# Full-height float32r products, with the weights' high and low parts on the two halves of the lanes, for the state products of the second four batches

## The chip, the cores and the metric

The kernel runs on one core of a Trainium2 chip. The metric is the device time of one execution in microseconds, the median of several runs. The time before is 1491.74 us, the median of 3 runs (1489.16 to 1493.12).

## The reference

Three layers follow each other, all in float32.

- Bidirectional attention between 8 batches of 512 tokens (`x`, 8 heads of 64) and, for each batch, 32 state rows (`state`, the same heads). Each token reads the states (softmax over the 32 states, then `a @ state`), and each state reads the tokens (softmax over the 512 tokens, then `a2 @ x`).
- A gated feed-forward layer on the 4352 rows that come out: `(silu(x @ w_gate) * (x @ w_val)) @ w_out`, 512 to 1536 to 512.
- A second one: `h = x @ w_in`, `(h * sigmoid(1.702 h)) @ w_out`, 512 to 2048 to 512.

What the tokens read is `a @ state` (per head), and the next layer multiplies it with `w_gate` and `w_val`. The kernel multiplies the states with those weights first, per batch and head: `a @ (state_h @ w_h)`, where `w_h` is the 64 rows of the weight that belong to head h.

## The kernel before, in words

**Exactness by parts.** The products are made in float32r, a form of float32 that TensorE multiplies in one pass. A number is split into a high part (a cast to float32r) and a low part (the number less its high part), and a product is the sum of three matmuls: high x high, low x high, high x low (`mm_rows`, L327 to L332; `mm_acc`, L339 to L342). Where plain float32 is used instead, a matmul is recorded as two instructions.

**Order of the work.** The first stage goes through nine blocks of tokens: batches 0 to 6, then the 256 state rows, then batch 7. For each block there are twelve steps f = 0 to 11 (128 columns of the 1536 each), written out by hand in `run`: the product for the gate (`product`, L974), Silu on ScalarE (L977), whatever is planned for place 0; the product for the value (L986), its multiplication with the Silu on VectorE (L992), whatever is planned for place 1; the split of the result h (`cut`, L797 on ScalarE and L798 on VectorE), the twelve output matmuls of the step before (`out1(f - 1)`, L952 to L954), whatever is planned for place 2. At f = 0 there is no step before, so there are no output matmuls. A product of a token block is six matmuls of 128 x 128 by 512 columns (L330 to L332, twice). Each engine works through its instructions in the order in which they are written here.

**Jobs.** For every batch the products `state_h @ w_h` are made once. This goes by fours: the states of four batches stand side by side as the 128 columns of the stationary operand (`quad_t[qd]`, 64 lanes for each of the two heads of a pair). A job `quad_job(qd, u, k)` multiplies them with a weight tile of two heads (128 lanes x 512 columns: u counts 256 columns of gate and of value, k the four pairs of heads). The two heads of a pair stand on the two halves of the lanes, so a job is two plain float32 matmuls of 64 lanes (L629), one for each half, into two PSUM tiles. There are 24 jobs for each four. Those of the first four are made in block 0. Those of the second four are made in blocks 1, 2 and 3, eight in each, at place 0 of f = 1, 2, 3, 5, 6, 7, 10 and 11 (`job_places`, L681: place n is f = n // 3, place n % 3). The two PSUM tiles are copied into one tile "qs" by ScalarE (L635) and VectorE (L636), and stored to DRAM two places later by a DMA that ScalarE issues (`move`, L652). Of the second four's jobs every third takes its "qs" tile from a ring of two kept for that, the others from a ring of four tiles named "raw" (RAWS = 4), which weights and results of blocks also use. The products are fetched per batch (`fetch`, L661, issued by ScalarE) and split by `cut_fetched`, high on ScalarE (L667) and low on GpSimd (L668), a step or two before the product that uses them.

**The second four's states** are turned at place 0 of f = 0 of block 1: `turn_states(1)`, four transposes into PSUM (L383) and a copy by VectorE into `quad_t[1]` (L385). There too the last block's results leave PSUM (L808, L809).

**Attention pieces** of the next batch lie between (`GROUP`, L58 to L71): transposes of x on TensorE (L432), copied by ScalarE (L440) and reduced to the low part by VectorE (L445), at place 1 of f = 0, 1, 5 and 6; scores (L452 to L455) at f = 1 and 6, places 1 and 2; `cut_x` on GpSimd (L481) at f = 2 and 7; `state_sum` (L582 to L591) after f = 4 and 9.

Of the kernel before, what the change touches and what calls it, by code (L numbers as in the profile page):

```python
# [9 lines left out]
F32R = mybir.dt.float32r  # L10
U32 = mybir.dt.uint32
ACTF = mybir.ActivationFunctionType
ALU = mybir.AluOpType
# [61 lines left out]
def kernel(  # L75
# [26 lines left out]
    DM = H * D  # L102
    FF1 = w_gate.shape[1]
    FF2 = w2_in.shape[1]
    P = 128
    KD = DM // P
# [4 lines left out]
    HP = H // 2  # L111
# [4 lines left out]
    v, a, pe, pool_e, sy = nc.vector, nc.scalar, nc.tensor, nc.gpsimd, nc.sync  # L116
# [4 lines left out]
    work = ctx.enter_context(tc.tile_pool(name="work", bufs=2))  # L121
# [5 lines left out]
    late = ExitStack()  # L127
# [3 lines left out]
    ap = early.enter_context(tc.tile_pool(name="attn", bufs=1))  # L131
# [4 lines left out]
    def f32(t):  # L136
        return t.bitcast(F32)
# [13 lines left out]
    whole = {}  # L151
# [4 lines left out]
    pos = {"dma": 0, "begun": 0, "done": 0, "ahead": 4, "outs": 0, "jobs": 0}  # L156
    RAWS = 4
# [127 lines left out]
    def need_whole(key):  # L285
        while pos["done"] <= where[key]:
            before = pos["done"], pos["begun"]
            whole_slot()
            assert before != (pos["done"], pos["begun"]), key
# [57 lines left out]
    def gv():  # L347
        return psg.tile([P, 512], F32, name="gv", tag="gv")
# [3 lines left out]
    def at():  # L352
        if extra:
            extra.append(extra.pop(0))
            if extra[0] != "at":
                return psa.tile([P, 512], F32, name="at", tag=extra[0])
        return pst.tile([P, 512], F32, name="at", tag="at")
# [3 lines left out]
    stc = ap.tile([P, HP, 2, 64], F32R, name="stc")  # L361
    v.memset(f32(stc), 0.0)
    quad_t = {}
    HALVES = [(slice(0, 64), slice(0, 32)), (slice(64, 128), slice(32, 64))]
    sread = dp.tile([NT, DM], F32, name="sread")

# [12 lines left out]
    def turn_states(qd):  # L379

        ps = at()
        for hp in range(HP):
            pe.transpose(ps[:, hp * P : (hp + 1) * P], sb["raw"][:, hp, :], ident)  # L383
        quad_t[qd] = t = ap.tile([P, HP, P], F32, name="qt", tag="qt", bufs=2)
        v.tensor_copy(t, ps.rearrange("p (k m) -> p k m", k=HP))  # L385

    def attn_state(b):
        t = quad_t[b // 4][:, :, b % 4 * NS : b % 4 * NS + NS]
        for r, c in HALVES:
            if b < 2:  # L390
                src = t[r].rearrange("p (g q) m -> p g q m", g=2)
                a.copy(sts[b][r, :, 0:3:2, c], src)
            else:
                a.copy(stc[r, :, 1, c], t[r])
        if b > 1:
            for r, c in HALVES:
                v.tensor_tensor(stc[r, :, 0, c], t[r], f32(stc[r, :, 1, c]), op=ALU.subtract)
# [222 lines left out]
    def quad_job(qd, u, k, late=False):  # L620


        if qd == 0:
            need_whole(("gv", u, k))
        w = whole[u * KD + k]
        ps = [at(), at()]
        for hl in range(2):
            r = slice(hl * 64, hl * 64 + 64)
            pe.matmul(ps[hl], quad_t[qd][r, k], w[r], start=True, stop=True)  # L629
        pos["jobs"] += 1  # L630
        if qd == 0 and not late or pos["jobs"] % 3 == 0:
            t = ap.tile([P, 2, DM], F32, name="qs", tag="qs", bufs=2)
        else:
            t = work.tile([P, 2, DM], F32, name="qs", tag="raw", bufs=RAWS)
        a.copy(t[:, 0], ps[0])  # L635
        v.tensor_copy(t[:, 1], ps[1])  # L636
        g, q = divmod(k, 2)
        skip = NS * (1 - qd)
        if q == 0:
            quads[qd, u, g] = dp.tile([4 * (P - skip), DM], F32, name=f"sw{qd}_{u}_{g}")  # L640
        rows = quads[qd, u, g].rearrange("(q h p) m -> q p h m", q=2, h=2)
        moved[qd].append((rows[q], t[skip:]))
        if qd == 0 and u >= OWN:
            if q == 0:
                sw[0, u, g] = x_tiles(xp, u % 2 * 2 + g, DM)
            for hl in range(2):
                r = slice(q * 64 + hl * NS, q * 64 + hl * NS + NS)
                sy.dma_start(f32(sw[0, u, g][0][r]), t[:NS, hl])

    def move():  # L650
        for to, t in moved.pop(0):
            a.dma_start(to, t)  # L652
        moved.append([])
# [17 lines left out]
    def job_places(b):  # L671

        if b == 0:
            own = [-2, 0, 1, 2]
            first = [(n, 0, k) for k, n in enumerate((0, 1, 2, 3))]
            last = [(n, 1, k) for k, n in enumerate((28, 30, 32, 34))]
            return [(n, 0, u, k) for n, u, k in first + last] + [
                (6 * (u - 1) + own[k], 0, u, k) for u in range(OWN, U1) for k in range(KD)
            ]
        if b < 4:  # L680
            return [(n, 1, *divmod(8 * (b - 1) + j, KD)) for j, n in enumerate((3, 6, 9, 15, 18, 21, 30, 33))]  # L681
        return []

    def plan_weights(plan, i):


        b = order1[i]
        nb = order1[i + 1] if i + 1 < NB1 else None
        if nb == B:
            nb = None  # L690

        def put(f, place, fn, *args):
            plan.setdefault((f, place), []).append(lambda: fn(*args))

        for n, qd, u, k in job_places(b):
            put(n // 3, n % 3, quad_job, qd, u, k, n >= 3 * F1 - 6)
        for g in range(2):
            if 0 < b < B:
                put(b == 1, g, cut_fetched, b, 1, g)
                if b == 1:  # L700
                    put(0, g + 1, fetch, b, 1, g)
                for u in range(2, U1):
                    put(2 * u - 3, g + 1, fetch, b, u, g)
                    put(2 * u - 2 + (b == B - 1), g + (b < B - 1), cut_fetched, b, u, g)
            if nb is not None:
                put(9, g, fetch, nb, 0, g)
                put(10, g, cut_fetched, nb, 0, g, (ae, f"a{g}") if b == B else None)
                if nb > 1:
                    put(11, g, fetch, nb, 1, g)
# [21 lines left out]
    def plan_batch(plan, b):  # L731

        G0 = groups[b, 0]
        G1 = groups[b, 1] = Group(b, 1, {"xn": "xc1"} if b < 2 else None, b < 2)

        def load_next():
            if b + 1 < B:
                groups[b + 1, 0] = Group(b + 1, 0)
                if b + 1 == 2:
                    load_states(1)  # L740
                groups[b + 1, 0].load()

        named = {"A0": A0, "A1": A1, "G0": G0, "G1": G1}
        more = {"attn_state": lambda: attn_state(b), "next": load_next}
        if b == 1:
            for key, words in BLOCK0.items():
                plan[key] = [piece(w, named, more) for w in words.split()]
            return
        plan[0, 0] = [lambda: attn_state(b)]
        if b == 2:  # L750
            plan[0, 0].append(lambda: turn_states(1))
        for g, f0, then in (("G0", 0, G1.load), ("G1", 5, load_next)):
            for (f, place), words in GROUP.items():
                fns = [then if w == "next" else piece(f"{g}.{w}", named, more) for w in words.split()]
                plan.setdefault((f0 + f, place), []).extend(fns)
        plan.setdefault((5, 0), []).append(G0.state_store)
        plan.setdefault((10, 0), []).append(G1.state_store)
# [42 lines left out]
    def x_tiles(pl, k, N):  # L800
        t = pl.tile([P, 2, S], F32R, name="xo", tag=f"x{k}")
        return t[:, 0, :N], t[:, 1, :N]
# [24 lines left out]
    def warm():  # L827
# [3 lines left out]

    more = {
        "attn_state": lambda: (turn_states(0), attn_state(0)),
        "slot": whole_slot,
        "sw0": lambda: state_weights(0, 0),
# [65 lines left out]
    for i, blk in enumerate(order1):  # L901
# [5 lines left out]
        if blk + 1 < B:  # L907
            plan_batch(plan, blk + 1)
        plan_weights(plan, i)
        if i == NB1 - 3:  # L910
            plan.setdefault((F1 - 2, 2), []).append(load_tail)
# [358 lines left out]
    for n in range(len(order2)):  # L1270
        N = NT if order2[n] == B else S
        for f in range(F2):
# [14 lines left out]
            ps = gv()  # L1287
# [43 lines left out]
```

## Time and profile before

| what | value |
|---|---|
| median of 3 runs | 1491.74 us (1489.16 to 1493.12) |
| the profiled execution | 1492.28 us |
| its span, first to last instruction | 1490.5 us |
| granted clock of TensorE, mean over the span | 0.997 of 2.4 GHz |
| TensorE busy | 1467.6 us, 7688 matmuls |
| VectorE, ScalarE, GpSimd busy | 915.6, 684.2, 396.1 us |
| data moved by DMA | 269.30 MB, mean 181 GB/s |

PE is TensorE's matmuls, PEld its weight loads (which overlap with matmuls), DVE is VectorE, ACT is ScalarE, POOL is GpSimd, SP is SyncE; a q behind an engine's name is its sequencer. Times of a timeline are microseconds from the start of the span. Matmuls are pipelined: one shown with 0.40 us lets the next start after a little over half of that, so what a matmul costs is read from start to start. In a timeline, instructions of one line that follow each other are merged into one row (x4).

### The profile page before, as it was taken

To read this page: it belongs to the slowest core of one execution; us is meant where nothing else is said; L and a number is where in the kernel's file an instruction comes from. 1 tells how busy PE (TensorE), PEld (TensorE's weight loads), DVE (VectorE), ACT (ScalarE), POOL (GpSimd) and SP (SyncE) were. 2 spreads that over 40 slices of the span, in tenths; PEclk is the share of its full clock that TensorE was granted. 3 is DMA by queue.
4 is the path that set the end of the run, shared out by engine and by line. 5 is a ranking of instruction groups with operands and counts; after the bars stand their busy time and mean duration, and the time that the engine had idled before them with its cause. 6 is when DMAs were issued, how large, how long until landed. Compare 5 with 4: busy or idle time off the path is not lost.

```text
span 1490.5 us, 21226 instructions
## 1 busy us (share of the span) xinstructions
PE 1467.6 (98%) x7688; PEld 1193.8 (80%) x7688; DVE 915.6 (61%) x1600; ACT 684.2 (46%) x1247; POOL 396.1 (27%) x325
## 2 busy tenths in 40 slices
PE   7999999999999999999999999999999999999998
PEld 4445677777787777898788889999999999999997
DVE  7985565656678787943344335656565665656554
ACT  6766554555566666654444333333333232323322
POOL 2665221222234445477646330000000000000000
PEclk9999999999999999999999999999999999999999
DMA  7975433333365656425657746565654646574653
GB/s 217 292 248 159 133 99 110 108 125 105 126 189 172 197 170 190 130 100 171 207 189 270 261 147 211 180 232 174 209 198 170 240 159 240 178 240 165 207 183 128
DMA packets 138480, 269.30 MB, mean 181 GB/s; under 512 B 46728, under 2 KB 57992, under 8 KB 138376
## 3 DMA queue, kind: packets, MB, share of 16 engines
q1 hardware_dynamic: 114680, 223.64, 45.5%
q10 hardware_dynamic: 23696, 44.31, 8.9%
q8 instruction: 61, 1.00, 0.3%
q14 instruction: 43, 0.35, 0.1%
HBM read 202.11 MB, written 63.70 MB: 178 GB/s over the span
## 4 chain that ended last, share of the span: by engine, by line
PE 84%; DMA 5%; DVE 4%; ACT 3%; issue 2%; POOL 1%; SPq 0%; ACTq 0%; DVEq 0%; POOLq 0%
PE acc L340 8%; PE acc L341 8%; PE acc L342 8%; PE acc L952 5%; PE acc L954 5%; PE gv L330 5%; PE acc L953 5%; PE gv L331 4%; PE gv L332 4%; DMA xf<-sw 4%; PE gv L1232 4%; PE gv L1231 4%; PE gv L1230 4%; PE at L629 4%; PE at L1230 3%; PE at L1231 3%
## 5 line engine op out<-in xcount | busy, mean ns | idle before, releaser
L798 DVE TENSOR_TENSOR h<-sg,h 128x512 fp32r<-128x512 f32 (+1 forms) x240 | 193.5, 806 | 129.8 <-ACT h L797 128.2
L797 ACT CAST h<-sg 128x512 fp32r<-128x512 f32 (+1 forms) x251 | 149.8, 597 | 170.4 <-DVE sg L1264 80.2
L340 PE MATMUL acc<-wo,h 128*128 128x512 f32 x512 | 200.6, 392 | 0.0
L341 PE MATMUL acc<-wo,h 128*128 128x512 f32 x512 | 200.6, 392 | 0.0
L342 PE MATMUL acc<-wo,h 128*128 128x512 f32 x512 | 199.2, 389 | 0.0
L1254 ACT ACTIVATE sg<-wt 128x512 f32<-128x512 f32 x56 | 35.4, 632 | 299.5 <-DVE wt L1252 299.5
L668 POOL TENSOR_TENSOR xo<-xf,xo 128x512 fp32r<-128x512 f32 x84 | 110.9, 1325 | 231.9 <-ACT xo L667 216.5
L952 PE MATMUL acc<-h,wu 128*128 128x512 f32 (+1 forms) x428 | 165.9, 388 | 0.1
L954 PE MATMUL acc<-h,wu 128*128 128x512 f32 (+1 forms) x428 | 163.8, 383 | 2.0 <-DVE h L798 2.0
L953 PE MATMUL acc<-h,wu 128*128 128x512 f32 (+1 forms) x428 | 163.4, 382 | 0.0
L330 PE MATMUL gv<-a,xo 128*128 128x512 f32 x336 | 137.3, 409 | 0.0
L331 PE MATMUL gv<-a,xo 128*128 128x512 f32 x336 | 133.9, 399 | 0.6 <-POOL xo L668 0.5
L332 PE MATMUL gv<-a,xo 128*128 128x512 f32 x336 | 133.0, 396 | 0.0
L992 DVE TENSOR_TENSOR sg<-gv,sg 128x512 f32<-128x512 f32 (+1 forms) x107 | 70.5, 659 | 83.1 <-PE gv L332 50.7
L342 PEld LDWEIGHTS acc<-wo,h 128*128 128x128 f32 x512 | 96.2, 188 | 20.8
L340 PEld LDWEIGHTS acc<-wo,h 128*128 128x128 f32 x512 | 96.6, 189 | 17.1
L341 PEld LDWEIGHTS acc<-wo,h 128*128 128x128 f32 x512 | 96.6, 189 | 15.8
L1252 DVE TENSOR_TENSOR wt<-wt,gv 128x256 f32<-128x256 f32 x56 | 23.6, 421 | 136.4 <-PE gv L1232 136.4
L952 PEld LDWEIGHTS acc<-h,wu 128*128 128x128 f32 x428 | 80.9, 189 | 22.1 <-issue 6.1
L977 ACT ACTIVATE sg<-gv 128x512 f32<-128x512 f32 (+1 forms) x108 | 61.5, 570 | 80.1 <-PE gv L332 77.0
L954 PEld LDWEIGHTS acc<-h,wu 128*128 128x128 f32 x428 | 80.9, 189 | 21.1 <-DVE h L798 5.5
L1232 PE MATMUL gv<-xo,wu 128*128 128x256 f32 x336 | 95.4, 284 | 0.0
(178 smaller groups left out, 3438.6 us busy)
## 6 DMA issues: line engine op xcount, KB each, us to landing
wo<-w2b SPq DMA_DIRECT2D x128, 512.0 KB
wc<-w2c SPq DMA_DIRECT2D x84, 512.0 KB
xf<-sw ACTq DMA_DIRECT2D x84, 256.0 KB
raw<-in_moe_w_out_dram SPq DMA_DIRECT2D x28, 512.0 KB
sw<-qs ACTq DMA_DIRECT2D x24, 512.0 KB
sw<-qs ACTq DMA_DIRECT2D x24, 384.0 KB
xn<-in_x_dram SPq DMA_DIRECT2D x16, 512.0 KB
y<-ev SPq DMA_DIRECT2D x16, 512.0 KB
```

The costliest lines, as they stand in the source:

```text
L330: pe.matmul(ps, wh, xh, start=k == 0, stop=False)
L331: pe.matmul(ps, wl, xh, start=False, stop=False)
L332: pe.matmul(ps, wh, xl, start=False, stop=k == len(pairs) - 1)
L340: pe.matmul(ps, lh, rh, start=first, stop=False)
L341: pe.matmul(ps, lh, rl, start=False, stop=False)
L342: pe.matmul(ps, ll, rh, start=False, stop=last)
L797: a.copy(h_, src)
L798: eng.tensor_tensor(l_, src, f32(h_), op=ALU.subtract)
L952: pe.matmul(ps, w[:, 0, c], h[:, 0, :N], start=f == 0, stop=False)
L953: pe.matmul(ps, w[:, 1, c], h[:, 0, :N], start=False, stop=False)
L954: pe.matmul(ps, w[:, 0, c], h[:, 1, :N], start=False, stop=f == F1 - 1)
L1232: pe.matmul(ps, w[:, 0, c], x_[:, 1, kt], start=False, stop=kt == 1)
```

## The change

The jobs of the second four batches are made as float32r matmuls of full height. The 64 rows of a head's weight appear twice on the 128 lanes: the high part on the head's own half, the low part on the other half. The states of that head appear twice as well, once on each half, as high parts (`sh`) and as low parts (`sl`). One matmul with `sh` gives high x high + high x low, one with `sl` low x high + low x low. So a job becomes four matmuls of 128 lanes, two for each head, in place of two plain float32 matmuls of 64 lanes.

`turn_states(1)` makes `sh` and `sl`, each 128 lanes x 1024 numbers, by four ScalarE copies and four VectorE subtractions over 64 lanes x 512; they take the two "qs" tiles, which the second four's jobs then no longer use: all their results go to the ring "raw". A new function `cut_job`, planned two places before each job (place 1 of f - 1), makes the weight's parts in another tile of that ring: two copies of 64 lanes x 512 by ScalarE and two subtractions by GpSimd, the second of each for the other head. The jobs of the first four stay as they were.

```diff
@@ -361,6 +361,8 @@
     v.memset(f32(stc), 0.0)
     quad_t = {}
+    quad_parts = []
+    job_parts = {}
...
@@ -383,6 +385,15 @@
         quad_t[qd] = t = ap.tile([P, HP, P], F32, name="qt", tag="qt", bufs=2)
         v.tensor_copy(t, ps.rearrange("p (k m) -> p k m", k=HP))
+        if qd == 1:
+            sh, sl = (ap.tile([P, HP, 2, P], F32R, name="qp", tag="qs", bufs=2) for _ in range(2))
+            for hl in range(2):
+                own, other = (slice(64 * x_, 64 * x_ + 64) for x_ in (hl, 1 - hl))
+                for r in (own, other):
+                    a.copy(sh[r, :, hl], t[own])
+                for r in (own, other):
+                    v.tensor_tensor(sl[r, :, hl], t[own], f32(sh[own, :, hl]), op=ALU.subtract)
+            quad_parts.extend((sh, sl))
...
@@ -624,11 +635,16 @@
         w = whole[u * KD + k]
         ps = [at(), at()]
+        wc = job_parts.pop((u, k)) if qd else None
         for hl in range(2):
             r = slice(hl * 64, hl * 64 + 64)
-            pe.matmul(ps[hl], quad_t[qd][r, k], w[r], start=True, stop=True)
+            if qd == 0:
+                pe.matmul(ps[hl], quad_t[qd][r, k], w[r], start=True, stop=True)
+                continue
+            for n, part in enumerate(quad_parts):
+                pe.matmul(ps[hl], part[:, k, hl], wc[:, hl], start=n == 0, stop=n == 1)
         pos["jobs"] += 1
-        if qd == 0 and not late or pos["jobs"] % 3 == 0:
+        if qd == 0 and (not late or pos["jobs"] % 3 == 0):
             t = ap.tile([P, 2, DM], F32, name="qs", tag="qs", bufs=2)
...
@@ -647,6 +663,14 @@
+    def cut_job(u, k):
+        w = whole[u * KD + k]
+        job_parts[u, k] = t = work.tile([P, 2, DM], F32R, name="wc", tag="raw", bufs=RAWS)
+        for hl in range(2):
+            own, other = (slice(64 * x_, 64 * x_ + 64) for x_ in (hl, 1 - hl))
+            a.copy(t[own, hl], w[own])
+            pool_e.tensor_tensor(t[other, hl], w[own], f32(t[own, hl]), op=ALU.subtract)
+
...
@@ -693,6 +717,8 @@
         for n, qd, u, k in job_places(b):
+            if qd == 1:
+                put((n - 2) // 3, (n - 2) % 3, cut_job, u, k)
             put(n // 3, n % 3, quad_job, qd, u, k, n >= 3 * F1 - 6)
```

## Rows read from the trace of the kernel before

**Rows 1.** The page: busy time by engine, and the chain that ended last.

```profile
PE 1467.6 (98%) x7688; PEld 1193.8 (80%) x7688; DVE 915.6 (61%) x1600; ACT 684.2 (46%) x1247; POOL 396.1 (27%) x325
...
PE 84%; DMA 5%; DVE 4%; ACT 3%; issue 2%; POOL 1%; SPq 0%; ACTq 0%; DVEq 0%; POOLq 0%
```

**Rows 2.** Windows, blocks 1 and 3: stretch, length, each engine's busy time (instructions), clock, DMA.

```profile
154.00:240.00 86.00, 85.53 (x369) 61.89 (x368) 53.70 (x90) 44.18 (x77) 22.65 (x17) 1.00 0.33 111
...
325.00:412.00 87.00, 87.00 (x379) 64.02 (x378) 54.29 (x91) 43.77 (x77) 21.27 (x16) 1.00 0.38 129
```

**Rows 3.** Groups by line, TensorE, 154 to 412: count | busy us, mean ns | idle.

```profile
L629 PE MATMUL at<-wf,qt 64*128 64x512 f32 x96 | 32.4, 639 | 0.0
```

**Rows 4.** Timeline around an ordinary job (f = 6, block 1): start, length, instruction.

```profile
199.83 0.40 PE L332 MATMUL gv<-a,xo 128*128 128x512 f32 x1
...
200.54 0.40 PE L332 MATMUL gv<-a,xo 128*128 128x512 f32 x1
200.87 1.13 PE L629 MATMUL at<-wf,qt 64*128 64x512 f32 x4
...
201.93 0.50 PE L330 MATMUL gv<-a,xo 128*128 128x512 f32 x1
...
202.26 0.40 PE L331 MATMUL gv<-a,xo 128*128 128x512 f32 x1
```

**Rows 5.** Timeline around a long job (f = 5, block 1), TensorE and VectorE.

```profile
192.25 1.25 DVE L587 TENSOR_TENSOR low<-at,low 64x128 f32<-64x128 f32 x4 [0.38 <-ACT low L582]
...
192.66 0.39 PE L332 MATMUL gv<-a,xo 128*128 128x512 f32 x1
192.98 1.76 PE L629 MATMUL at<-wf,qt 64*128 64x512 f32 x4
...
194.67 0.49 PE L330 MATMUL gv<-a,xo 128*128 128x512 f32 x1
```

**Rows 6.** Single lines, 154 to 412: count, shortest/median/longest ns, first and last start, shape.

```profile
L668 POOL TENSOR_TENSOR xo<-xf,xo x36: 1265/1288/1312, 167.2 to 401.9; 128x512 fp32r<-128x512 f32 x36
...
L481 POOL TENSOR_TENSOR xc<-xn,xc x12: 1289/1570/1737, 177.2 to 384.8; 128x512 fp32r<-128x512 f32 x12
...
L454 ACT COPY ST<-at x12: 581/582/583, 167.7 to 377.5; 64x512 f32<-64x512 f32 x12
...
L455 DVE TENSOR_TENSOR ST<-at,ST x12: 682/683/685, 168.3 to 378.1; 64x512 f32<-64x512 f32 x12
```

**Rows 7.** Timeline of the start of block 1, up to its first job.

```profile
160.09 0.69 DVE L385 COPY qt<-at 128x512 f32<-128x512 f32 x1
...
161.01 0.59 ACT L440 CAST xth<-at 128x512 fp32r<-128x512 f32 x1 [1.86 <-PE at L432]
...
162.30 1.20 PE L629 MATMUL at<-wf,qt 64*128 64x512 f32 x4
```

**Rows 8.** Timeline of the start of block 2, up to its first job.

```profile
247.63 0.59 ACT L440 CAST xth<-at 128x512 fp32r<-128x512 f32 x1 [0.78 <-PE at L432]
...
248.11 0.62 ACT L667 CAST xo<-xf 128x512 fp32r<-128x512 f32 x1
...
248.87 1.27 POOL L668 TENSOR_TENSOR xo<-xf,xo 128x512 fp32r<-128x512 f32 x1 [0.59 <-ACT xo L667]
248.92 1.19 PE L629 MATMUL at<-wf,qt 64*128 64x512 f32 x4
```

**Rows 9.** Timeline of ScalarE before the job of rows 4.

```profile
196.80 0.59 ACT L440 CAST xth<-at 128x512 fp32r<-128x512 f32 x1 [2.08 <-PE at L432]
```

**Rows 10.** Timeline of block 2, f = 7: GpSimd and VectorE at the same time.

```profile
298.73 2.99 POOL L481 TENSOR_TENSOR xc<-xn,xc 128x512 fp32r<-128x512 f32 x2 [3.49 <-ACT xc L480]
298.78 1.79 DVE L798 TENSOR_TENSOR h<-sg,h 128x512 fp32r<-128x512 f32 x1
```

**Rows 11.** Timeline of block 1, f = 1 and 2.

```profile
169.14 0.47 PE L452 MATMUL at<-xth,stc 128*128 128x512 f32 x1 [0.37 <-DVE ST L455]
...
169.80 1.30 POOL L668 TENSOR_TENSOR xo<-xf,xo 128x512 fp32r<-128x512 f32 x1
```

## The prediction

> **What bounds the kernel now.** I read the page first: TensorE is busy 98% of the span, and the chain that ended last lies on it for 84% [rows 1]. The profiled execution took 1492.28 us (span 1490.5), 0.54 us above the median of the three runs; I make the sum against 1492.28 and take 0.5 off at the end. Then the stretches in which the change acts, blocks 1 to 3 of the first stage, 154 to 412 us: TensorE is busy for nearly all of each block, ScalarE for half, GpSimd for a quarter [rows 2]. So here a microsecond taken from TensorE's instructions is a microsecond of the end, one that TensorE waits is lost, and work added to ScalarE or GpSimd is free only while its result is ready when TensorE reaches the job that uses it. That last question decides this case.
>
> **What is removed.** The 24 jobs of these blocks keep TensorE busy for 32.4 us [rows 3]. An ordinary job: matmuls of 512 columns follow each other at 0.237 us (199.83 to 200.54 in three steps); from the last one before the job (200.54) to the second after it (202.26) is 1.72 us, so the job costs 1.72 - 2 x 0.237 = 1.25, which is 0.12 more than its busy 1.13: the edges between half-height and full-height work [rows 4]. All jobs: 32.4 + 24 x 0.12 = 35.3 us. Seven of them are long (1.69 instead of 1.06 from first start to the next line's): the second head's PSUM bank is freed only when VectorE's L587 group ends at 193.50 [rows 5].
>
> **What comes in its place on TensorE**: 96 full-height float32r matmuls of 512 columns, the form of L330 to L332, so 24 x 4 x 0.237 = 22.8 us. Gain 35.3 - 22.8 = **12.5 us**. Against this speaks a rule of the Trainium skill (TensorEngine Tiling (Array Packing), Theoretical Speedup): a contraction of 64 or less gains up to 2x from two row tiles, which the change gives up; a half-height pair side by side here takes 0.53, and if a full-height matmul cost as much, the gain would turn into a loss of some 16 us. The trace does not agree for float32r: L330's takes 0.237.
>
> The long jobs keep part of their wait, since the bank is released by others. In the one shown the job would start 0.09 earlier (no edge), its first two matmuls end at 193.36, and the second pair could start some 0.14 after 193.50: 0.28 us. Over the seven (0.24 to 0.48 each by how long they last) that is **2.4 us** given back; bounds 0 and 3.5.
>
> **What is added**, and where it lies.
> - Each job gets two ScalarE copies and two GpSimd subtractions, each over 64 lanes x 512, two places before the job. No GpSimd row has 64 lanes. GpSimd's full-height subtraction L668 takes 1.288 us in the median; on ScalarE and VectorE half-height rows (L454, L455) cost 0.58 and 0.68, what full-height ones cost (0.59, 0.69) [rows 6, 7]. By these I take 1.29 for GpSimd; bounds are half of it (0.64) if it goes by lanes, and 1.74, the slowest of the pairs L481. Together 48 x 1.29 = 62 us of GpSimd and 48 x 0.58 = 28 us of ScalarE, which fit into their idle time as sums.
> - Once, at the start of block 1, four ScalarE copies and four VectorE subtractions cut the states, between VectorE's L385 and L992.
> - No DMA is added. The fetches that ScalarE issues (L661) go behind the copies, about a microsecond later. The eight products that lay in the tile "qs" go to the ring of four that also takes the weight parts; there a job reuses what the job two before it left, some 14 us earlier, and the store of a product is issued two places behind it. I cost that at nothing; without that cover it would be a store's landing per job.
>
> **When is the weight part ready?** The copies go on ScalarE behind what its place has already, at f - 1, place 1; the job is at f, place 0. Between the two TensorE normally has the twelve output matmuls of place 2 (12 x 0.237 = 2.8 us) and one product (six, 1.4). At f = 6, ScalarE starts L440 at 196.80 [rows 9] and can follow 0.49 later: copies done 197.89 and 198.4, GpSimd (0.14 later, as in [rows 8]) 198.03 to 199.3 and on to 200.6. The second pair is due at 200.87 - 0.09 + 0.475 = 201.25: in time by 0.65. f = 2 and f = 7 are alike, the others looser. **But at f = 0 there are no output matmuls.** So the first job of each block, three in all, comes too early:
> - Block 2: L440 starts at 247.63, the copy follows at 248.12 and ends at 248.72, GpSimd works 248.87 to 250.15 and to 251.45; the second pair then ends at 251.93, where a job with all at hand would end at 248.92 - 0.09 + 0.95 = 249.78 [rows 8]. TensorE loses 2.15 us. Block 3 has the same order and loses 2.4.
> - Block 1: after L385 (ends 160.78) the four state copies hold ScalarE until 162.9, so L440, at 161.01 now, starts at 162.8 and the weight copies at 163.3; VectorE's subtractions run until 164.3; GpSimd works 164.04 to 166.6, or until 166.9 if VectorE holds it up. The job ends near 167.4 instead of 162.30 - 0.09 + 0.95 = 163.16 [rows 7]: 4.25 us.
> Together **8.8 us** lost; by the two bounds of GpSimd's instruction (six of them stand in these waits) 4.9 and 11.5.
>
> What is late next, in block 1 only: GpSimd's second L668 there, now at 169.80, is wanted by the product at f = 2 almost at once [rows 11]. It goes behind one more pair of GpSimd subtractions (2.6 us), while TensorE comes 4.25 later and the DMA that feeds this chain is not as much later. I put 1.5 us of wait, less 0.4 that TensorE now waits before L452 at 169.14 and then no longer would: **1.1 us**, bounds -0.4 and 2.6.
>
> VectorE and GpSimd hold each other up: while GpSimd's pair L481 ran (2.99 us instead of 2 x 1.29), VectorE's L798 took 1.79, where its like alone take 0.69 [rows 10]. VectorE's delays are covered (h is wanted 5 us later). GpSimd's 0.41 per pair eats most of the margin at f = 2, 6 and 7: **0.4 us** over these eight jobs, bounds 0 and 3. The Trainium skill (SBUF — State Buffer, Who interferes with whom) has this as an exclusive lock for a whole instruction, so that one 0.69 us subtraction of VectorE could slip in between the pair: 0.69 instead of 0.41, which would make the 0.4 about 1.0. The row shows less.
>
> **Sum**: 12.5 - 2.4 - 8.8 - 1.1 - 0.4 = -0.2 us: the gain is all but used up. 1492.28 + 0.2, less 0.5 for the median: **1491.9 us**.
>
> **Rivals.**
> - *Faster: the cuts are cheap.* If a half-height GpSimd instruction takes 0.64, the three block starts lose 4.9, L668's wait and the interference vanish: 12.5 - 2.4 - 4.9 = 5.2, 1486.6 us. For it: half the elements. Against it: the half-height rows of the two other engines. 0.14.
> - *Slower: the cuts are late at more than the block starts.* If each takes 1.74 in the middle of VectorE's work, as the slowest of L481 do, the starts lose 2.7 more, L668's wait 0.9, and f = 2, 6 and 7, whose margins I put at 0.65 to 0.9, some 3.9 less the 0.4: 7.1 more, 1499.0 us. It decides from about 1.57 us an instruction (then the loss passes 4.5). For it: L481's median, 1.57. Against it: L668 never exceeds 1.312 beside the same VectorE [rows 6]. 0.17.
> - *The new matmuls are no cheaper than the old*: no gain, but the costs, 1492.28 + 8.8 + 1.1 + 0.4 - 0.5 = 1502 us. Only if float32r products of this kind differ from L330's. 0.04. The skill's rule on row tiles, taken at its word, adds the 16 us named above.
>
> **How the numbers follow.** The forecast, no change that can be told (0.3% is 4.5 us here, about what a measurement can tell), has 0.65; its own range is 1488 to 1496. Faster by over 0.3% is the first rival, 0.14; slower the other two, 0.21. The range reaches to the first two: 1485.5 to 1499.
>
> **What would show it.** Right: L629's line has 96 matmuls of 128 lanes, 0.237 apart, with no edges; TensorE idles before it three times, at f = 1 of blocks 1 to 3, released by GpSimd's subtraction, 4 us once and 2 us twice; GpSimd's new line near 1.29 us; the three blocks together as long as before. Wrong: waits on GpSimd in more than a few other jobs (slower), starts that lose under a microsecond (faster), or the time moving outside these blocks, for which I see no reason.

## The result, and the profile after

The changed kernel takes **1505.93 us** (median; 1503.39 to 1514.12), the one before 1491.71 beside it: ratio 1.0106, 95% interval 1.0089 to 1.0123. It is slower by 14 us. The forecast was no change, 1491.9 us with a range up to 1499.0; the result lies 7 us above the range. The profiled execution took 1506.14 us, its span is 1504.3, the mean granted clock 0.992.

The page of the changed kernel: busy time by engine, and the chain that ended last.

```profile
PE 1462.7 (97%) x7688; PEld 1207.1 (80%) x7688; DVE 934.4 (62%) x1604; ACT 713.1 (47%) x1299; POOL 465.6 (31%) x373
...
PE 70%; DMA 7%; ACT 4%; DVE 3%; issue 2%; POOL 2%; ACTq 0%; SPq 0%; POOLq 0%; DVEq 0%
```

TensorE is busy for 4.9 us less than in [rows 1], but the span is 13.8 longer: TensorE now waits, and its share of the chain falls from 84% to 70%.

Windows of the changed kernel, blocks 1 to 3; the columns are those of [rows 2].

```profile
154.00:240.00 86.00, 76.98 (x340) 60.82 (x340) 58.57 (x90) 52.97 (x93) 44.62 (x33) 0.96 0.32 102
240.00:325.00 85.00, 79.87 (x360) 63.45 (x359) 56.82 (x90) 52.27 (x92) 42.65 (x31) 1.00 0.34 113
325.00:412.00 87.00, 81.87 (x363) 65.10 (x361) 56.60 (x89) 51.25 (x91) 42.65 (x32) 0.98 0.33 110
```

TensorE is idle for 9 us in the first window (0.5 in the same window before), 5 in each of the others. GpSimd works twice as long, ScalarE 7 to 9 us longer, and the clock column falls to 0.96 and 0.98.

**The matmuls are as cheap as forecast.** Timeline of the changed kernel, the job at f = 2 of block 1 (no job waits there):

```profile
176.85 0.39 PE L332 MATMUL gv<-a,xo 128*128 128x512 f32 x1
177.08 1.10 PE L645 MATMUL at<-wc,qp 128*128 128x512 f32 x4
178.02 0.39 PE L330 MATMUL gv<-a,xo 128*128 128x512 f32 x1
```

L645 is the jobs' new line. From its first start to the next line's, 177.08 to 178.02, the job takes 0.94 us and has no edges. Counted as the forecast counts, from the last matmul before the job to the second one behind it, less two (at 0.235), such a job takes 0.927 in place of 1.25; times of jobs below and their excess over 0.927 are counted so.

**What TensorE waits for.** The waits between 150 and 430 us: engine and line, releaser, us in total, times, the longest.

```profile
PE at L645 <- POOL wc L672: 7.7, 6, 3.6
PE at L645 <- ACT qs L651: 5.3, 3, 1.9
PE at L645 <- DVE low L598: 2.1, 2, 1.1
PE gv L331 <- POOL xo L692: 1.7, 1, 1.7
PE at L645 <- ACT xo L691: 1.3, 1, 1.3
PE at L645 <- DVE ST L466: 1.1, 3, 0.4
```

There are four kinds. *The weights' parts at the block starts* (L672 is `cut_job` on GpSimd). Timeline of block 2's first job, ScalarE, GpSimd and TensorE:

```profile
253.15 1.26 ACT L671 CAST wc<-wf 64x512 fp32r<-64x512 f32 x2
...
253.91 2.61 POOL L672 TENSOR_TENSOR wc<-wf,wc 64x512 fp32r<-64x512 f32 x2 [0.66 <-ACT wc L671]
255.22 0.30 PEld L645 LDWEIGHTS at<-wc,qp 128*128 128x128 f32 x2 [1.63 <-POOL wc L672]
255.22 0.73 PE L645 MATMUL at<-wc,qp 128*128 128x512 f32 x2 [1.18 <-POOL wc L672]
...
256.57 0.73 PE L645 MATMUL at<-wc,qp 128*128 128x512 f32 x2 [0.62 <-POOL wc L672]
```

The pair of GpSimd instructions takes 2.61 us; TensorE starts the first half as the first ends, waits again for the second, and the job takes 2.34 us more than 0.927.

*The second halves of jobs* (L651, L598, L691, L466 in the list: PSUM copies and what they stand behind). Timeline of the job at f = 5, block 1, which answers to [rows 5]:

```profile
192.00 2.67 POOL L672 TENSOR_TENSOR wc<-wf,wc 64x512 fp32r<-64x512 f32 x2 [4.39 <-issue]
...
194.75 1.36 POOL L692 TENSOR_TENSOR xo<-xf,xo 128x512 fp32r<-128x512 f32 x1
194.99 1.66 DVE L545 TENSOR_TENSOR a<-aT,a 128x512 fp32r<-128x512 f32 x1
...
197.05 0.63 PE L645 MATMUL at<-wc,qp 128*128 128x512 f32 x2
...
197.43 1.25 DVE L598 TENSOR_TENSOR low<-at,low 64x128 f32<-64x128 f32 x4
197.52 0.62 ACT L691 CAST xo<-xf 128x512 fp32r<-128x512 f32 x1 [1.14 <-DMA xf<-sw]
198.04 0.59 ACT L1003 ACTIVATE sg<-gv 128x512 f32<-128x512 f32 x1
...
198.53 0.58 ACT L651 COPY qs<-at 128x512 f32<-128x512 f32 x1
...
199.25 0.71 PE L645 MATMUL at<-wc,qp 128*128 128x512 f32 x2 [1.58 <-ACT qs L651]
```

Before, the group now at L598 began 0.73 us ahead of the job, now 0.38 after it: VectorE is late. And the second half waits not for that group but for L651, the copy of the job's own *first* half: the two halves have got the same one of the two PSUM tiles (read from the releaser here; the run with strict turns below bears it out). That copy in turn stands in ScalarE's order behind Silu (L1003) and behind L691, which waits 1.14 us for the DMA of the fetched rows; in blocks 2 and 3 it is the same, with 1.50 and 1.38 us.

*`cut_fetched` in block 1* (L692): 1.7 us once.

*A wait that was in no part of the forecast*, at the start of block 4. Timeline of ScalarE and TensorE:

```profile
420.66 0.36 ACTq L676 DMA_DIRECT2D sw<-qs  x1
...
430.11 0.59 ACT L834 COPY ev<-acc 128x512 f32<-128x512 f32 x1 [4.80 <-DMA sw<-qs]
...
432.31 0.60 PE L330 MATMUL gv<-a,xo 128*128 128x512 f32 x1 [2.31 <-DVE sg L1018]
```

The copy of the last block's results wants a tile of the ring of four. It holds the last job's product, whose store was issued at 420.66 and ends only at 430. ScalarE waits 4.80 us, and behind it TensorE.

**The clock.** Windows of three stretches of the changed kernel, with the granted clock behind the engines:

```profile
162.90:169.70 6.80, 4.98 (x11) 3.49 (x12) 2.36 (x4) 3.31 (x6) 5.43 (x4) 0.50 0.19 64
343.80:347.20 3.40, 3.33 (x8) 2.66 (x9) 1.26 (x2) 0.07 (x1) 1.63 (x2) 0.50 0.00 0
432.60:436.00 3.40, 3.40 (x10) 2.51 (x10) 2.75 (x3) 2.48 (x6) 1.86 (x2) 0.51 0.97 280
```

At 0.50 (1.2 of 2.4 GHz) the full-height matmuls start 0.427 us apart in place of 0.233. All three stretches begin in or right behind waits of blocks 1, 3 and 4; a fourth is at 565.7 to 569.1. Before there was none in blocks 1 to 5.

From first result copy to first result copy, block 1 takes 93.81 us (87.05 before), block 2 87.29 (84.87), block 3 88.68 (84.87), block 4 78.81 (75.58), block 5 77.41 (77.32): 16.3 us more. What lies before and behind gives 2.4 back, between two executions.

### The profile page after: what moved, and what is told of

Same layout as the page of the kernel before. It is cut to its first block, busy times and chain, and to the rows that moved or that the text cites. A ratio compares the mean times of both kernels' runs of the same rounds, so it can differ in the third digit from the quotient of the medians.

```text
span 1504.3 us, 21367 instructions
## 1 busy us (share of the span) xinstructions
PE 1462.7 (97%) x7688; PEld 1207.1 (80%) x7688; DVE 934.4 (62%) x1604; ACT 713.1 (47%) x1299; POOL 465.6 (31%) x373
## 4 chain that ended last, share of the span: by engine, by line
PE 70%; DMA 7%; ACT 4%; DVE 3%; issue 2%; POOL 2%; ACTq 0%; SPq 0%; POOLq 0%; DVEq 0%
PE acc L340 8%; PE acc L341 8%; PE acc L342 8%; DMA xf<-sw 5%; PE gv L1258 4%; PE gv L1257 4%; PE gv L1256 4%; PE gv L331 3%; PE gv L332 3%; PE gv L330 3%; PE acc L980 3%; PE acc L979 3%; PE acc L978 3%; PE at L1256 3%; PE at L1257 3%; PE at L1258 3%
## 5 line engine op out<-in xcount | busy, mean ns | idle before, releaser
L692 POOL TENSOR_TENSOR xo<-xf,xo 128x512 fp32r<-128x512 f32 x84 | 115.2, 1376 | 108.5 <-ACT xo L691 98.3
L1003 ACT ACTIVATE sg<-gv 128x512 f32<-128x512 f32 (+1 forms) x108 | 61.7, 571 | 71.2 <-PE gv L332 68.0
```

## The experiments

Diffs are against the changed kernel unless said otherwise. "Second-half wait" is what lies between a job's second and third matmul beyond 0.235 us, from start to start.

**The two halves of the change.** *Without the weights' cuts*; the states' high parts stand in as the moving operand.

```diff
-        wc = job_parts.pop((u, k)) if qd else None
+        wc = quad_parts[0].rearrange("p k h m -> p (k h m)").rearrange("p (h m) -> p h m", h=2) if qd else None
...
-            if qd == 1:
-                put((n - 2) // 3, (n - 2) % 3, cut_job, u, k)
```

> Leaves out the weights' high and low parts altogether: the 96 full-height matmuls of blocks 1 to 3 take the states' high parts as their moving operand too, so the products are not those of the reference; the states are still cut at the start of block 1. Theory A (what cost the time are the cuts: GpSimd's subtractions are late at the block starts and hold VectorE up, so that PSUM banks come free late): no wait on GpSimd before a job, the waits before a job's second half fall from 11.9 us to the 2 to 3 us that the old form had, block 1's start keeps about 2 us for the states' low parts, TensorE's clock stays up, and the time is 13 us of cheaper matmuls less some 5: about 1484 us (1481 to 1487). Theory B (the waits before the second half come from the new matmuls themselves, which reach the bank sooner and at f = 5 share the first half's bank): those waits stay at 8 to 12 us, and the time is 1490 to 1494.

Measured: 1485.2 us, ratio 0.9955 (0.9941 to 0.9969). Blocks 1 to 3 take 86.33, 82.35 and 82.13. So the matmuls alone do gain, 7 us; two costs stay without any weight cut. Its waits, 154 to 412 us:

```profile
PE at L645 <- ACT qs L651: 2.5, 3, 1.0
PE at L645 <- DVE xtl L456: 1.5, 1, 1.5
PE at L645 <- ACT qp L393: 1.0, 1, 1.0
```

The first row is the shared PSUM tile at f = 5 (second-half waits of 0.9 to 1.2 each). The others are block 1's first job behind the states' cut.

*All cuts made, but the products by the old half-height matmuls*:

```diff
-            if qd == 0:
+            if True:
                 pe.matmul(ps[hl], quad_t[qd][r, k], w[r], start=True, stop=True)
```

> All cuts are made, but the jobs go back to the old half-height float32 matmuls, which do not use them. Theory A: no wait on GpSimd's parts at the block starts; the waits before a job's second half rise from 2.5 us toward the changed kernel's 11.9 (VectorE is late by GpSimd's work), and the evacuation at the start of block 4 still waits for the ring: 1497 to 1503 us. Theory B (the new matmuls make the waits): the second halves wait as in the kernel before, and the time is within 3 us of it plus block 4's 2 to 4 us, 1492 to 1496.

Measured: 1504.98 us, ratio 1.0088 (1.0071 to 1.0106), above both. The cuts cost 12 us although no job uses them: long jobs take 2.75 to 3.05 us (1.87 and 2.05 before), those at f = 7 2.05 (1.29), and the first job of block 1 5.77, at half clock. Timeline at f = 5 of block 1 (the old matmuls are L642 here):

```profile
198.47 1.12 PE L642 MATMUL at<-wf,qt 64*128 64x512 f32 x2
...
198.77 1.25 DVE L598 TENSOR_TENSOR low<-at,low 64x128 f32<-64x128 f32 x4
...
200.16 1.09 PE L642 MATMUL at<-wf,qt 64*128 64x512 f32 x2 [0.57 <-ACT sg L1003]
```

VectorE's group begins 0.30 us behind the job, where it began 0.73 ahead of it before, and the second half starts 0.14 after that group's end. So a loss of this size comes about without TensorE waiting for a single weight part, through VectorE, ScalarE and the PSUM tiles.

**One cost at a time.** *A block's first cut in the block before*:

```diff
-            if qd == 1:
+            if qd == 1 and n > 3:
                 put((n - 2) // 3, (n - 2) % 3, cut_job, u, k)
...
+        if b < 3:
+            put(F1 - 1, 1, cut_job, *divmod(8 * b, KD))
```

> Only the cut of each block's first job is moved, to the last step of the block before (f = 11, place 1). Theory A: the waits on GpSimd before the first jobs of blocks 2 and 3 (1.35 + 0.78 us each) are gone, and with them the half clock in block 3; in block 1 the states' low parts, ready near 162.6, still hold the job for about 2 us; 8 to 11 us less than the changed kernel, 1495 to 1498. If the half clock does not follow from these waits but from the work, it stays (7 us of half clock in block 1, 3.4 in block 3) and the gain is 5 to 6 us, 1500.

Measured: 1498.76 us, ratio 1.0036 (1.0022 to 1.005), 7 us less. In blocks 2 and 3 the first job takes 0.92 and 0.93 us, no wait left. In block 1 it still takes 3.99: its second half waits 2.5 us, now for VectorE's L456 (the low part of x) behind the states' cut. The block starts were a real cost, and in block 1 it was the states' cut as much as the weights'.

*The low parts by VectorE* (`v` for `pool_e` in `cut_job`):

> The changed kernel with the weights' low parts made by VectorE in place of GpSimd (0.69 us instead of 1.29, and no GpSimd beside it). If the two engines' hold on each other is what makes the second halves wait, those waits fall from 11.9 us toward the 4 to 5 us of the run without cuts, the parts at the block starts are ready 1.2 us sooner, three times, and the time is 1492 to 1497. If it is only that VectorE has more to do, or is late for other reasons, its 33 us of added work keep the waits near 10 us: 1499 to 1504.

Measured: 1496.86 us, ratio 1.0046 (1.0029 to 1.0064). One group of VectorE, `a`'s low part, blocks 1 to 3; columns: instruction, count, busy us, mean ns, idle. In the changed kernel, then with the cuts on VectorE:

```profile
L545 DVE TENSOR_TENSOR a<-aT,a 128x512 fp32r<-128x512 f32 x6 | 10.0, 1662 | 0.2
```

```profile
L545 DVE TENSOR_TENSOR a<-aT,a 128x512 fp32r<-128x512 f32 x6 | 4.2, 692 | 0.2
```

The same instruction takes 1662 ns beside a GpSimd subtraction (a weight's, or the fetched rows' that now stands behind it) and 692 without, as before the change. In the timeline above it starts at 194.99 and ends at 196.65, 0.54 after GpSimd's L692 has ended. This is the first part of VectorE's delay at f = 5 and 10. But the waits do not fall with it; 150 to 430 us:

```profile
PE at L645 <- DVE wc L672: 6.9, 6, 4.1
PE at L645 <- ACT qs L651: 5.8, 6, 1.5
PE at L645 <- DVE ST L466: 1.0, 3, 0.3
```

Apart from each block's first job, second halves wait 10.6 us in all, 11.3 in the changed kernel: less at f = 5 (0.9 to 1.7) and f = 10 (0.86), more at f = 3 (1.1, 0.4, 0.4). So on the waits the rival was right, although the time lies in the theory's range. What is gained lies elsewhere: the block starts lose 7.9 us for 11.1, and blocks 4 and 5 take 75.6 and 73.6 for 78.8 and 77.4. GpSimd's hold on VectorE's instruction is shown; what share of the waits it makes is not, since VectorE's 48 added instructions come in its place.

*The PSUM tiles strictly in turn*:

```diff
-        return pst.tile([P, 512], F32, name="at", tag="at")
+        pos["at"] = 1 - pos.get("at", 0)
+        return pst.tile([P, 512], F32, name="at", tag=f"at{pos['at']}", bufs=1)
```

> The changed kernel with the two PSUM tiles that jobs and attention pieces share given out strictly in turn, so that at f = 5 the second half of a job no longer takes the tile of its first half. Theory A (VectorE, held up by GpSimd, frees the other tile late): the three waits there fall only from 1.7 to 2.1 us to 1.0 to 1.4 us, some 2 us in all, 1502 to 1506. Rival (the shared tile alone makes them): they fall to the 0.3 us that the old form had, 5 us in all or more with the clock, 1498 to 1501.

Measured: 1506.25 us, ratio 1.0105 (1.0088 to 1.0121), no gain as a whole. Timeline at f = 5 of block 1 (the jobs are L646 here, the group L599):

```profile
199.00 0.63 PE L646 MATMUL at<-wc,qp 128*128 128x512 f32 x2
...
200.78 0.70 PE L646 MATMUL at<-wc,qp 128*128 128x512 f32 x2 [1.16 <-DVE low L599]
```

The wait for the job's own copy is gone, that for VectorE's group takes its place: 1.3 us in each of the three, in place of 1.7 to 2.1. So sharing cost 0.4 to 0.8 each, VectorE's lateness the rest. The 2 us that this saves do not show in the whole; in the profiled execution the clock falls once more, at the start of block 2, and not in block 5.

*Without the early fetch of the next weights at block 3's end* (`w_dma(2)` removed there):

> The changed kernel without the two weight loads that take tiles of the ring at the end of block 3. If the wait of 2.5 us at the start of block 4 (ScalarE's evacuation waits for the store of the last product, and TensorE for the multiplication behind it) comes from the ring of four being full, it goes, and with it 3.4 us of half clock: 3 to 4 us less, 1502, unless the later loads make block 4 wait elsewhere by as much. If the store itself is late whatever the ring holds, the wait stays and the time is 1505 to 1507.

Measured: 1506.73 us, ratio 1.0098 (1.0081 to 1.0115). The wait at 430 goes, but some 10 us into the block TensorE loses 1.8 us at L463, waiting for `ST`, and block 4 gains 2.0 of the 3.2 us; the whole gains nothing. So this did not tell whether the store is the cause. *One job of block 3 alone moved from step 30 to step 24* does:

```diff
-            return [(n, 1, *divmod(8 * (b - 1) + j, KD)) for j, n in enumerate((3, 6, 9, 15, 18, 21, 30, 33))]
+            return [(n, 1, *divmod(8 * (b - 1) + j, KD)) for j, n in enumerate((3, 6, 9, 15, 18, 21, 30 if b < 3 else 24, 33))]
```

> The changed kernel with one job of block 3 moved: the seventh stands after step 24 in place of 30, so that only one product is on its way to DRAM when block 4's first result needs a tile of the ring. Theory (the ring's late stores cost block 4 its time): block 4 takes 75.5 to 76 us in place of 78.8, the clock does not fall at its start, and the whole is 2.5 to 4 us shorter than the changed kernel, 1502 to 1503.5 us. Rival (the wait belongs to what the tiles carry next and only moves, as without the early weights): blocks 4 and 5 together stay at 156 us, the whole at 1505 to 1507 us.

Measured: 1502.13 us, ratio 1.006 (1.0037 to 1.0084). Block 4 takes 74.84 us, 4.0 less, with no stretch at half clock. Its ScalarE still waits for the store, but only:

```profile
427.98 0.59 ACT L834 COPY ev<-acc 128x512 f32<-128x512 f32 x1 [2.23 <-DMA sw<-qs]
```

and TensorE has work for that long. The late stores of the last products were the cause of block 4's wait. Of the 3.8 us of the whole not all is theirs: the moved job no longer waits at f = 10 either (1.3 us), and block 3 takes 87.31 for 88.68.

**Other places for the jobs.** *Step 15 to 13 and 30 to 24 in all three blocks*:

```diff
-            return [(n, 1, *divmod(8 * (b - 1) + j, KD)) for j, n in enumerate((3, 6, 9, 15, 18, 21, 30, 33))]
+            return [(n, 1, *divmod(8 * (b - 1) + j, KD)) for j, n in enumerate((3, 6, 9, 13, 18, 21, 24, 33))]
```

> The changed kernel with two jobs of each block moved away from the state sums: from f = 5 to f = 4, place 1, and from f = 10 to f = 8, place 0. If the long waits before second halves come from the PSUM tile that the state sum still holds, the six (10.1 us in all) go, with little in their place: 1495 to 1498. If VectorE is late everywhere, the jobs wait at their new places too: 1501 to 1505.

Measured: 1497.36 us, ratio 1.0044 (1.0027 to 1.0061). Second-half waits: 0.93 at step 13, none at 24; block 4 takes 75.51.

*All remedies together*: first cuts early, the states' cut put off to places 2 of f = 0 and 0 of f = 1, block 1 without its first place, and other steps.

```diff
...
+            ns = (3, 6, 9, 13, 18, 21, 24, 28) if b > 1 else (6, 9, 13, 18, 21, 24, 28, 33)
...
+        if 0 < b < 3:
+            put(F1 - 1, 1, cut_job, *divmod(8 * b, KD))
+        if b == 1:
+            put(0, 2, cut_states)
+            put(1, 0, cut_states)
```

> The new matmuls with every wait found so far taken out of the way: first cuts of blocks 2 and 3 in the block before, the states' cut in two parts behind the first output of block 1, block 1 without a job at f = 1, jobs moved away from the state sums and from the end of block 3. If these waits (11 us at the starts, 10 at the state sums, 4 at block 4, 4 of half clock) are all that ate the 13 us of cheaper matmuls, about 1480 to 1485 us, clearly faster than the kernel before. If GpSimd's added work costs by itself, whatever the places, 1487 to 1493.

Measured: 1490.7 us, ratio 0.9987 (0.9975 to 1.0000): as fast as before, blocks 2 and 3 at 83.56 us. Waits remain at steps 13 (0.93), 21 (0.55) and 28 (1.2), and in block 1, where TensorE stands 2.1 us at the scores (L469).

*Steps 11 and 26 in place of the late ones, nine jobs in blocks 2 and 3, six in block 1*, and the states' cut a step later (against all remedies together):

```diff
+            ns = (3, 6, 9, 11, 18, 21, 24, 26, 33) if b > 1 else (9, 11, 18, 24, 26, 33)
...
+            put(1, 2, cut_states)
+            put(2, 0, cut_states)
```

> As the run that takes the waits out together, but the jobs lie at the places at which no run so far showed a wait (f = 1 with an early cut, 2, 3 at places 0 and 2, 6, 8 at places 0 and 2, 11; f = 7 in blocks 2 and 3 alone), six in block 1 and nine in blocks 2 and 3, and the states are cut at the end of f = 1 and at f = 2. If the waits are all that is between the cheaper matmuls and the clock on the wall, blocks 2 and 3 take 81 to 82 us and the time is 1480 to 1485. If the cuts cost something at whatever place (VectorE and ScalarE late for the attention pieces), new waits appear at scores, sums or transposes and the time is 1486 to 1492.

Measured: 1501.02 us, ratio 1.0056 (1.0043 to 1.0069). A miss: the cuts for steps 11 and 26 stand behind the softmax work of ScalarE, and TensorE loses 2.1 us or more waiting for GpSimd at each of these six jobs. *The same with the low parts by VectorE*:

> The same places with the weights' low parts made by VectorE in place of GpSimd. If GpSimd's hold on VectorE's two-input instructions is still felt there, this is 1 to 4 us faster than its pair; if VectorE's own queue is what counts, 1 to 4 us slower.

Measured: 1489.58 us, ratio 0.9989 (0.998 to 0.9999). 11 us less, where 1 to 4 were expected: none of the jobs at steps 11 and 26 waits any more; blocks 2 and 3 take 83.9.

*Steps free of all of these* (against all remedies together), and then also the PSUM tiles in turn:

```diff
+            ns = (3, 6, 9, 18, 21, 24, 31, 33) if b > 1 else (6, 9, 13, 18, 21, 24, 31, 33)
```

> The first cuts early, the states' cut split and block 1 without its first place, as in the run of all remedies together, but the places are moved off the three that still waited: after steps 3, 6, 9, 18, 21, 24, 31, 33 of a block in place of 3, 6, 9, 13, 18, 21, 24, 28. Theory (only waits stand between the cheaper matmuls and the wall time): blocks 2 and 3 take 81 to 82 us where that run had 83.6, and the whole 1484 to 1488 us. Rival (ScalarE and VectorE, loaded with copies and cuts, come late wherever the jobs stand): other jobs wait in place of those three, blocks stay at 83 to 85 us and the whole at 1489 to 1493 us.

> The same as the run with free places, and the two PSUM tiles of the products are given strictly in turn. Theory that a job whose halves share one tile still waits: the waits of second halves on ScalarE's copy go, and 0.5 to 1 us for each such job is saved against the run with free places: 1483 to 1488 us. Rival (no job's halves share a tile late enough to matter at these places): within 1 us of the run with free places.

Measured: 1488.76 us, ratio 0.9973 (0.9962 to 0.9983), and in turn 1489.7, 0.9982 (0.9971 to 0.9993). In both, blocks 2 and 3 take 82.3 us, near the theory; but with two products in flight at block 3's end, block 4 takes 79.26 and 80.22. The turns take the wait at step 13 of block 1 away and change no more than that, as the rival said. *The last, with block 3's seventh job back at step 13*:

```diff
+            ns = (3, 6, 9, 13, 18, 21, 24, 33) if b > 2 else (3, 6, 9, 18, 21, 24, 31, 33) if b > 1 else (6, 9, 13, 18, 21, 24, 31, 33)
```

> The run with free places and strict turns, but in block 3 the seventh job stands after step 13 in place of 31. Theory (late stores): block 4 takes 75.3 to 76 us in place of 80.2, block 3 stays at 82 to 82.5 us, and the whole is 1484 to 1486.5 us, 0.4% to 0.5% below the kernel before. Rival (the wait only moves on to block 5 and behind): the whole stays at 1488 to 1490 us.

Measured: **1485.07 us**, ratio 0.9954 (0.9939 to 0.9969): faster than the kernel before and 21 us below the changed one. Blocks 1 to 4 take 86.86, 82.32, 81.43 and 75.11. Its windows, columns as above, and its waits in 150 to 430 us:

```profile
154.00:240.00 86.00, 83.01 (x370) 66.23 (x369) 62.59 (x95) 57.10 (x99) 47.74 (x35) 0.98 0.34 110
240.00:325.00 85.00, 84.01 (x381) 67.76 (x380) 59.42 (x91) 52.63 (x93) 45.32 (x33) 1.00 0.36 120
325.00:412.00 87.00, 86.63 (x395) 70.18 (x394) 58.24 (x95) 54.14 (x97) 42.48 (x31) 1.00 0.40 134
```

```profile
PE at L470 <- DVE ST L473: 2.0, 1, 2.0
PE at L649 <- DVE srd L593: 1.4, 1, 1.4
PE at L652 <- POOL wc L679: 1.2, 2, 0.6
PE at L652 <- DVE ST L473: 1.1, 3, 0.4
```

GpSimd and ScalarE are as busy as in the changed kernel, yet TensorE's idle time in the second and third window falls from 5.1 us to 1.0 and 0.4. The load of the cuts can stay; what cost the time was where it stood. Whether the kernel before would gain from the same places with its old matmuls, whose long jobs waited too, was not tried; so the 7 us below it are not all shown to be the new matmuls'.

## Why the prediction was wrong

The forecast's terms, and what the changed trace shows, from start to start:

| term | forecast, us | measured, us |
|---|---|---|
| matmuls of the jobs | 12.5 gained | 13.0 gained (35.3 - 24 x 0.927) |
| long jobs' second halves | 2.4 lost | 11.9 lost |
| block starts | 8.8 lost | 11.1 lost, half clock within them included |
| L692 in block 1 | 1.1 lost | 1.9 lost |
| GpSimd and VectorE at other jobs | 0.4 lost | 0 |
| ring of four, block 4 | 0 | 2.5 lost |
| clock outside the jobs | not counted | 4.6 lost |
| other waits of blocks 1, 4 and 5 | 0 | 2.8 gained |

The measured column sums to 16.2 lost; the five blocks are 16.3 longer. The whole lies above even the slowest rival's 1502.

**The step that failed most** is "The long jobs keep part of their wait, since the bank is released by others", with 0.24 to 0.48 us each and a bound of 3.5 in all. Nine second halves wait: by the jobs' excess over 0.927, 2.0 us each at f = 5, 1.4 at f = 10, 0.6 at f = 7 (1.81 + 2.17 + 2.06, 1.54 + 1.19 + 1.38, 0.60 + 0.58 + 0.59). Two things failed. First, the step took the release time from the trace of before, while the change puts GpSimd and ScalarE work ahead of just those releases. The prediction had the mechanism (GpSimd's instruction holds up VectorE's, [rows 10]) and put it aside with "VectorE's delays are covered (h is wanted 5 us later)". h is covered; the PSUM release that stands behind it in VectorE's order is not. The run with the cuts alone shows this. What part of it is GpSimd's hold on VectorE, and what part the added work of ScalarE and GpSimd itself, stays open: with the cuts on VectorE the second halves wait nearly as long. Second, it assumed that the two halves still have a PSUM tile each; that at f = 5 the second half would get the first half's tile was not seen, and the run with strict turns shows what it costs, 0.4 to 0.8 each.

L545 pays 0.97 us for one GpSimd instruction (1662 ns against 692) and ends 0.54 us after it. [rows 10] had this price too: there VectorE's L798 pays 1.10 (1.79 against 0.69) and ends at 300.57, 0.55 after the first of the pair (1.295 of its 2.99 us). The prediction took from these rows only what GpSimd pays, 0.41 us a pair, and put VectorE's part at nothing. The Trainium skill (SBUF — State Buffer, Who interferes with whom) says that a VectorE instruction with two inputs in SBUF and a GpSimd instruction that reads SBUF exclude each other for a whole instruction. The trace agrees but for some 0.15 us: shut out until GpSimd's end, L545 would end 0.69 after it.

**The ring at nothing** failed too. "A job reuses what the job two before it left" holds within a block. At block 4's start the ring's next user is the copy of results, and the store ends 9.4 us after its issue. The step looked at jobs only, not at the tile's other users; moving one job gave 4.0 us of block 4 back.

**The clock** was not a term. Four stretches at 1.2 GHz cost 1.05, 0.86, 1.34 and 1.34 us on matmuls of 512 columns outside the jobs (the one right behind a job counts with the job), and part of the first jobs of blocks 1 and 3.

**Right**: the matmuls; GpSimd's price for 64 lanes (1.29 forecast; the pair in block 2 takes 2.61, the median of all 48 is 1295 ns and the mean 1389, 1.74 was not needed); the block starts by place, releaser and size (2.34 in block 2 for 2.15, 2.99 in block 3 for 2.4, 5.74 in block 1 for 4.25, where half clock makes most of the difference); L692. The slower rival had cuts that come late at f = 2, 6 and 7 through slow GpSimd instructions; that did not happen. The time went where the sentence on the long jobs had it, at five times its price.

What stays open: why the effects of single parts don't add up. The matmuls alone give 7 us, the cuts alone cost 12, and together the change costs 14 in place of 5. Block 4's start (3.2 us, in neither part alone) is one piece; the rest, second halves that wait longer because a shorter job comes earlier to the same release, is argued from the timelines, not tried by itself.

## What to carry to other kernels

Work moved to idle engines is not free when these also release the bottleneck's buffers: follow each release that the bottleneck waits for back along its engine's order, and count what the change puts ahead of it. Do this for every user of a buffer ring, also the one in the next stage. Where the bottleneck then waits in a few places, moving jobs and their cuts by a few steps can be worth more than the arithmetic: here 21 us against 13.

## What was not expected of the hardware

- Equal waits do not always cost the same. At the starts of blocks 2 and 3 TensorE waits 1.18 and 0.62, and 1.19 and 0.62 us, in the same order of instructions; behind the second the granted clock is 0.50 from 343.8 to 347.2, behind the first it stays at 1.00. Block 3's, beside the rows of block 2 above:

```profile
342.51 0.74 PE L645 MATMUL at<-wc,qp 128*128 128x512 f32 x2 [1.19 <-POOL wc L672]
343.87 1.22 PE L645 MATMUL at<-wc,qp 128*128 128x512 f32 x2 [0.62 <-POOL wc L672]
```

- A GpSimd subtraction of 64 lanes takes what one of 128 lanes takes: 1389 ns in the mean for L672, 1400 for L692, 512 numbers in a lane both times. Groups by line, 154 to 430 us: count, busy us, mean ns, idle time and its releasers.

```profile
L672 POOL TENSOR_TENSOR wc<-wf,wc 64x512 fp32r<-64x512 f32 x48 | 66.7, 1389 | 75.3 <-ACT wc L671 39.8 <-issue 33.4
L692 POOL TENSOR_TENSOR xo<-xf,xo 128x512 fp32r<-128x512 f32 x36 | 50.2, 1400 | 48.6 <-ACT xo L691 47.0 <-DVE sq L524 0.4
```

- A VectorE subtraction of 128 x 512 takes 692 ns alone and 1662 beside one GpSimd subtraction.
